# Attention's instructions within the expert steps get scheduler numbers 150 lower

## The chip, the cores and the metric

The kernel runs on one core of a Trainium2 chip. The metric is the device time of one execution in microseconds (us); the figure for a kernel is the median of its runs.

## The reference

Three layers run one after the other on 4 x 576 = 2304 tokens of 512 features. q, k and v come as 4 batches of 8 heads, 576 positions and 64 features.

```python
# 1 attention in a window of 64 positions
scores = q @ k.T / 8;  mask = (0 <= i - j < 64);  attn = softmax(scores where mask)
x = attn @ v                                   # heads side by side: 2304 x 512
# 2 first expert: w_in 512 x 2048, w_out 2048 x 512
h = x @ w_in
g = where(h >= 1, h, where(h <= -1, 0, (h + 1)**2 / 4))
x = g @ w_out
# 3 second expert: w_in 512 x 1024, w_out 1024 x 512
h = x @ w_in2;  s = h * softmax(h);  ln = (s - mean(s)) / sqrt(var(s) + 1e-6) * g_ln
out = ln @ w_out2
```

The weights `w_in` and `w_out` of both experts come as 64-bit numbers, everything else as float32.

## The kernel before

**Number format.** Every matmul of the two experts is made of three, with each operand split into a high and a low part (`xh`, `xl`; `wih`, `wil`; `woh`, `wol`; `gh`, `gl`): high x high, high x low, low x high. The 64-bit weights arrive in staging tiles `wst` (five of them) and are converted by five operations: L132 and L145 on ScalarE, L136, L137 and L146 on VectorE (`split_a`, `split_b`, `split_c`).

**Attention.** Tokens are cut into 12 tiles of 192 (index t). Up to t = 3 and a little beyond, the unit of work is a tile and two of the eight heads (index g, four units to a tile); later it is a pair of such units (index P). A unit goes through stages: q and k are loaded (`load_qk`, 8 transfers on SP's queue from t = 3 on, before that by whole tiles) and put into one of two buffers `kq` (`st_qkt`, by TensorE transposes for t < 3, by VectorE later); scores (`st_s`, `pair_s`: TensorE L352 or L442, then VectorE L360 or L452 for mask and maximum and ScalarE L366 or L458 for the exponential and its sum); normalising (`st_norm`, VectorE L377 to L386); transposes (`st_t`, TensorE L400 and L402, copied by ScalarE to `pT`); values (`st_v`, `pair_v`: TensorE L421 or L476, then ScalarE writes `xh` and VectorE `xl`, L428 and L429 or L483 and L484). In block 0 attention has two PSUM banks of its own and the experts' `ps_h` two; from block 1 on they share a ring of four. `p` has three buffers, `pT` two.

**First expert.** Tokens are taken in 6 blocks of 384 (index j), that is two tiles, and the hidden features in 16 groups of 128 (index f). A step (j, f) is 12 matmuls into `ps_h` (`moe_h`, L496, which read `xh[j]` and `xl[j]`), five operations for the activation (`moe_g`, `moe_g2`, `moe_g3`: ScalarE L505, L506, L512, VectorE L511, L515) and 12 matmuls into four accumulators (`moe_y`, L526), which are written in the program two steps later. At the end of a block the accumulators go to memory (`moe_out`). `xh` and `xl` have two buffers each, for the block in work and the next one. Block 0 is started in halves: its first two groups are done for its first 192 tokens, then for the other 192.

**How the two are interleaved.** The first seven units of attention are traced before the experts. The rest is a generator, `slots()`, which yields after each small stage. The step loop calls `slot(n0)` after a step's `moe_h` and `slot(n1)` after its `moe_y`; both are one slot in most steps, and eight slots are spread over the first two half steps. So a unit takes four slots, or two steps; a pair takes eight slots, or four steps. The last values stage for block 1 (unit 15) is the 38th of the 40 slots that fall in block 0. In block 0 each step also holds two weight conversions (`w_conv`) and two weight loads (`w_load`, SP's queue).

**What sets the order.** The kernel is written in Tile: the program as traced gives each instruction a number, and a scheduler fixes beforehand each engine's own order. Among the instructions of an engine whose inputs and buffers it takes to be ready, it picks the lowest number. On the chip each engine, and each DMA queue, keeps to the order so fixed. A few instructions are tied to others by hand (`tc.issue_after`).

**Second expert.** During blocks 1 to 5 its weights are converted as well (`w2_step`, partly on GpSimd). It begins inside block 5 and is alone from about 525 us on (the last L526 starts at 525.0).

Of the kernel before, what the change touches and what calls it, by code (L numbers as in the profile page):

```python
# [20 lines left out]
def kernel(  # L21
# [578 lines left out]
    def slots():  # L600
        for g in range(G0 + 1, GB + 1):
            st_s(g)
            yield
            st_v(g - 1)
            st_norm(g)
            yield
            qkt_and_loads(g + 1)
            v_ahead(g)
            yield
            st_t(g)  # L610
            if g == GB:
                st_s(g + 1)
            yield
        st_norm(GB + 1)
        qkt_and_loads(2 * PU)
        yield
        st_v(GB)
        st_t(GB + 1)
        qkt_and_loads(2 * PU + 1)
        yield  # L620
        for P in range(PU, NPP + 1):
            if P == PU:
                st_v(GB + 1)
            else:
                pair_v(P - 1)
            if P % NPR == 0:
                v_ahead(2 * P)
            if P < NPP:
                pair_s(P)
            yield  # L630
            if P < NPP:
                st_norm(P, 0)
                st_norm(P, 1)
            yield
            qkt_and_loads(2 * P + 2)
            yield
            qkt_and_loads(2 * P + 3)
            yield
            yield
            yield  # L640
            if P < NPP:
                st_t(P, 0)
                st_t(P, 1)
            yield
            yield

    stages = slots()

    def slot(n):
        for _ in range(n):  # L650
            next(stages, None)

    TPN = NB // 128
    NK2 = DF2 // 128
# [192 lines left out]
    for n in range(len(seq) + 2):  # L847
# [29 lines left out]
        if n < len(seq):  # L877
            prev = part
            slot(n0)
            w_conv()  # L880
            pins = moe_g2(*part)
# [5 lines left out]
        if n < len(seq):  # L887
            slot(n1)
            w_conv()
            if j == 0:  # L890
                w_load(2)
            w2_step(n, *pins)
            if last and f < 2:
                w2_vals(f)
            if last and f in (2, 3):
                w2_sums(f - 2)
            if last and f >= 2:
                with tc.issue_after(pins[0]):
                    w2_split(f - 2)
            if last and 2 <= f < 10:  # L900
                w2_load(f - 2)
        else:
            w_conv()
# [82 lines left out]
```

## Time and profile before

| | |
|---|---|
| median of 3 runs | 709.37 us (708.8 to 710.54) |
| the profiled execution | 709.96 us, span 708.2 us, mean granted TensorE clock 0.99 |
| TensorE matmuls (PE) | busy 683.4 us (96%), 4439 instructions |
| TensorE weight loads (PEld) | 629.5 us (89%) |
| VectorE (DVE) | 446.9 us (63%) |
| ScalarE (ACT) | 411.8 us (58%) |
| GpSimd (POOL) | 116.1 us (16%) |

The profile is of one execution. Its span goes from the first to the last instruction; the execution's own time is 1.8 us longer. Busy time is the share in which an engine works on an instruction; matmuls overlap each other and their weight loads, so a busy TensorE says that it had work, not that it ran at its peak. The granted clock is the share of full speed that TensorE was given: 1.00 is 2.4 GHz, 0.5 is 1.2 GHz. SP is the engine that issues most transfers.

### The profile page before, as it was taken

To read this page: it belongs to the slowest core of one execution; us is meant where nothing else is said; L and a number is where in the kernel's file an instruction comes from. 1 tells how busy PE (TensorE), PEld (TensorE's weight loads), DVE (VectorE), ACT (ScalarE), POOL (GpSimd) and SP (SyncE) were. 2 spreads that over 40 slices of the span, in tenths; PEclk is the share of its full clock that TensorE was granted. 3 is DMA by queue.
4 is the path that set the end of the run, shared out by engine and by line. 5 is a ranking of instruction groups with operands and counts; after the bars stand their busy time and mean duration, and the time that the engine had idled before them with its cause. 6 is when DMAs were issued, how large, how long until landed. Compare 5 with 4: busy or idle time off the path is not lost.

```text
span 708.2 us, 12544 instructions
## 1 busy us (share of the span) xinstructions
PE 683.4 (96%) x4439; PEld 629.5 (89%) x4439; DVE 446.9 (63%) x1213; ACT 411.8 (58%) x1006; POOL 116.1 (16%) x151
## 2 busy tenths in 40 slices
PE   6899898899999999999999999999999999999998
PEld 5799787799999999999999999999987788888887
DVE  4789788655545544454555543642379999988850
ACT  5889667465656555566666665364454646445451
POOL 1000000100001000021111200662272222220000
PEclk9999999899999999999999999999999999999999
DMA  9996787624343623447342211553024455533331
GB/s 199 224 259 193 193 213 199 154 40 105 71 107 79 148 60 67 80 104 148 96 89 81 85 60 60 171 180 110 1 84 140 149 187 163 188 132 133 120 105 45
DMA packets 155543, 88.94 MB, mean 126 GB/s; under 512 B 118616, under 2 KB 141400, under 8 KB 155480
## 3 DMA queue, kind: packets, MB, share of 16 engines
q1 hardware_dynamic: 144040, 64.00, 36.5%
q0 software_dynamic: 8704, 19.41, 8.4%
q10 hardware_dynamic: 2736, 4.72, 1.8%
q8 instruction: 35, 0.57, 0.3%
q14 instruction: 28, 0.23, 0.1%
HBM read 63.97 MB, written 24.12 MB: 124 GB/s over the span
## 4 chain that ended last, share of the span: by engine, by line
PE 75%; DVE 9%; issue 5%; DMA 4%; ACT 4%; POOL 2%; SPq 0%; DVEq 0%; POOLq 0%; ACTq 0%
PE ps_h L496 23%; PE acc L526 22%; PE ps_o L825 13%; PE P L710 8%; DMA wst<-in_moe_w_out_dram 2%; PE ps_x L476 2%; POOL wil L249 2%; PE ps_p L402 2%; PE ps_s L442 2%; PE ps_s L352 2%; DVE gl L515 1%; DVE wst L137 1%; ACT p L366 1%; DMA wst<-in_moe_w_in_dram 1%; PE ps_x L421 1%
## 5 line engine op out<-in xcount | busy, mean ns | idle before, releaser
L511 DVE SCALAR_TENSOR_TENSOR u<-u,ps_h 128x384 f32<-128x384 f32 (+1 forms) x98 | 53.2, 543 | 140.7 <-ACT u L506 139.7
L496 PE MATMUL ps_h<-xh,wih 128*128 128x384 f32 (+1 forms) x392 | 132.7, 339 | 1.3 <-DVE u L511 0.9
L526 PE MATMUL acc<-gl,woh 128*128 128x384 f32 (+1 forms) x392 | 130.6, 334 | 2.3 <-DVE gl L515 2.3
L496 PE MATMUL ps_h<-xl,wih 128*128 128x384 f32 (+1 forms) x392 | 131.7, 336 | 0.5 <-DVE xl L429 0.4
L496 PE MATMUL ps_h<-xh,wil 128*128 128x384 f32 (+1 forms) x392 | 132.0, 337 | 0.1
L526 PE MATMUL acc<-gh,wol 128*128 128x384 f32 (+1 forms) x392 | 129.5, 332 | 0.0
L526 PE MATMUL acc<-gh,woh 128*128 128x384 f32 (+1 forms) x392 | 125.3, 343 | 3.3 <-ACT gh L512 3.3
L505 ACT ACTIVATE u<-ps_h,half 128x384 f32<-128x384 f32 (+1 forms) x98 | 56.1, 573 | 95.2 <-PE ps_h L496 95.0
L515 DVE TENSOR_TENSOR gl<-u,gh 128x384 fp32r<-128x384 f32 (+1 forms) x98 | 61.3, 627 | 37.6 <-ACT gh L512 37.1
L512 ACT CAST gh<-u 128x384 fp32r<-128x384 f32 (+1 forms) x98 | 49.6, 507 | 51.4 <-DVE u L511 34.1
L526 PEld LDWEIGHTS acc<-gh,woh 128*128 128x128 f32 x392 | 72.2, 188 | 6.8 <-ACT gh L512 3.8
L496 PEld LDWEIGHTS ps_h<-xh,wih 128*128 128x128 f32 x392 | 74.9, 191 | 2.4 <-DVE u L511 1.1
L526 PEld LDWEIGHTS acc<-gl,woh 128*128 128x128 f32 x392 | 73.7, 188 | 3.6 <-DVE gl L515 3.4
L496 PEld LDWEIGHTS ps_h<-xl,wih 128*128 128x128 f32 x392 | 74.9, 191 | 1.0 <-DVE xl L429 0.8
L496 PEld LDWEIGHTS ps_h<-xh,wil 128*128 128x128 f32 x392 | 74.9, 191 | 0.8 <-DVE wil L146 0.7
L526 PEld LDWEIGHTS acc<-gh,wol 128*128 128x128 f32 x392 | 73.6, 188 | 0.1
L710 PE MATMUL P<-wih,x2p 128*128 128x512 f32 x216 | 70.7, 391 | 1.4 <-DVE xo L538 0.9
L825 PE MATMUL ps_o<-woh,wol 128*128 128x512 f32 (+1 forms) x152 | 57.7, 380 | 0.3 <-DVE wol L813 0.3
L825 PE MATMUL ps_o<-woh,woh 128*128 128x512 f32 (+1 forms) x152 | 57.7, 379 | 0.0
L825 PE MATMUL ps_o<-wol,woh 128*128 128x512 f32 (+1 forms) x152 | 57.5, 378 | 0.0
L506 ACT ACTIVATE u<-u 128x384 f32<-128x384 f32 (+1 forms) x98 | 51.0, 520 | 2.0
L710 PEld LDWEIGHTS P<-wih,x2p 128*128 128x128 f32 x216 | 40.5, 188 | 10.4 <-DVE xo L538 1.3
(122 smaller groups left out, 1175.9 us busy)
## 6 DMA issues: line engine op xcount, KB each, us to landing
vw<-in_v_dram SPq DMA_DIRECT2D x32, 256.0 KB, 5.2
wst<-in_moe_w_in_dram SPq DMA_DIRECT2D x16, 512.0 KB, 5.7
wst<-in_moe_w_out_dram SPq DMA_DIRECT2D x16, 512.0 KB, 5.3
lnd<-e SPq DMA_DIRECT2D x16, 512.0 KB, 2.6
lT<-lnd SPq DMA_DIRECT2D x64, 128.0 KB, 3.0
x2d<-xo POOLq DMA_DIRECT2D x24, 192.0 KB, 2.7
out_dram<-o ACTq DMA_DIRECT2D x17, 256.0 KB, 2.0
wst<-in_moe_w_in_dram POOLq DMA_DIRECT2D x8, 512.0 KB, 5.4
```

The source lines that it names most:

```text
L249: nc.gpsimd.tensor_tensor(lo, v_, as_f32(hi), op=ALU.subtract)
L352: nc.tensor.matmul(ps[:, i * 128 + c0:i * 128 + 128], qT[g][:, i, :, :].rearrange("p x q -> p (x q)"), kT[g][:, i * 64 + c0:i * 64 + 128], ...
L402: nc.tensor.transpose(ps[:, i * 128:i * 128 + 128], p[:, i, :], ident)
L496: nc.tensor.matmul(ps, a, bb[:, kc, c], start=(n == 0), stop=(n == 3 * KC - 1))
L505: nc.scalar.activation(u, ps, ACTF.Relu, bias=half, scale=0.5)
L506: nc.scalar.activation(u, u, ACTF.Square)
L511: g = nc.vector.scalar_tensor_tensor(u, u, 1.0, ps, op0=ALU.min, op1=ALU.max)
L512: return nc.scalar.copy(hi, u).ins, g.ins
L515: nc.vector.tensor_tensor(lo, u, as_f32(hi), op=ALU.subtract)
L526: nc.tensor.matmul(acc[j, e][:, c], a, bb, start=(f == 0 and n == 0 and c.start == 0), stop=(f == NF - 1 and n == 2),)
L710: nc.tensor.matmul(ps, l, r, start=(n == 0), stop=(n == 5))
L825: nc.tensor.matmul(ps, a[kk // 4][:, kk % 4, :], b[kk][:, c:c + w], start=(n == 0), stop=(n == 3 * NK2 - 1),)
```

## The change

`tc.high_priority(150)` lowers the number from which the scheduler counts by 150 for what is traced inside it, and puts it back on leaving. It is set around each slot of attention in the step loop. The stages of the first seven units, traced before the loop, are left as they are, and so is everything on GpSimd.

```diff
     def slot(n):
         for _ in range(n):
-            next(stages, None)
+            with tc.high_priority(150):
+                next(stages, None)
```

## Rows read from the trace of the kernel before

**Rows 1.** Stretches: us; busy PE, PEld, DVE, ACT, POOL (instructions); granted clock; DMA share; GB/s.
```profile
25.00:60.00 35.00, 31.80 (x279) 29.14 (x277) 29.97 (x100) 31.21 (x97) 0.00 (x0) 0.95 0.96 229
60.00:130.00 70.00, 63.38 (x403) 58.75 (x402) 58.45 (x164) 51.55 (x129) 1.25 (x2) 0.98 0.71 182
130.00:142.00 12.00, 9.17 (x57) 7.79 (x56) 6.79 (x29) 4.92 (x21) 2.70 (x5) 0.72 0.87 211
136.00:142.00 6.00, 5.75 (x21) 5.52 (x21) 2.29 (x11) 1.74 (x7) 0.34 (x1) 0.51 1.12 273
142.00:430.00 288.00, 288.00 (x2243) 278.78 (x2243) 148.81 (x480) 174.73 (x462) 32.44 (x47) 1.00 0.38 89
430.00:545.00 115.00, 112.24 (x624) 106.04 (x623) 61.46 (x102) 55.01 (x106) 50.71 (x50) 1.00 0.33 106
```
**Rows 2.** TensorE in order of time, 130 to 151 us: start, us, instruction, [idle before].
```profile
130.45 0.71 PE L421 MATMUL ps_x<-pT,vw 64*64 64x64 f32 x12
...
132.84 0.71 PE L421 MATMUL ps_x<-pT,vw 64*64 64x64 f32 x12
136.25 0.87 PE L402 MATMUL ps_p<-ident,p 128*128 128x128 f32 x3 [2.70 <-DVE p L386]
...
138.06 0.67 PE L496 MATMUL ps_h<-xh,wih 128*128 128x384 f32 x1
...
142.08 0.57 PE L421 MATMUL ps_x<-pT,vw 128*64 128x64 f32 x12
...
148.31 0.33 PE L496 MATMUL ps_h<-xh,wih 128*128 128x384 f32 x1
...
150.39 0.34 PE L526 MATMUL acc<-gl,woh 128*128 128x384 f32 x1
```
**Rows 3.** TensorE in order of time, three earlier places.
```profile
46.79 0.45 PE L496 MATMUL ps_h<-xh,wih 128*128 128x384 f32 x1 [0.91 <-DVE u L511]
...
119.07 0.83 PE L352 MATMUL ps_s<-kq 128*128 128x64 f32 x6
...
127.38 0.83 PE L352 MATMUL ps_s<-kq 128*128 128x64 f32 x6
```
**Rows 4.** Groups by line, ScalarE, whole span: count | busy us, mean ns | idle before.
```profile
L407 ACT COPY pT<-ps_p 128x384 f32<-128x384 f32 (+1 forms) x48 | 21.0, 440 | 2.4 <-PE ps_p L402 2.4
L366 ACT ACTIVATE p<-p,mx 128x128 f32<-128x128 f32 (+1 forms) x54 | 20.9, 390 | 5.0 <-DVE mx L360 4.9
...
L366 ACT ACTIVATION_READ_ACCUMULATOR p<-p,mx 128x1 f32 x54 | 10.4, 193 | 0.0
...
L428 ACT CAST xh<-ps_x 128x192 fp32r<-128x192 f32 x18 | 5.7, 314 | 0.9 <-PE ps_x L421 0.7
...
L339 ACT COPY kq<-ps_t 128x256 f32<-128x256 f32 (+1 forms) x12 | 4.3, 355 | 0.2
...
L338 ACT COPY kq<-ps_t 64x192 f32<-64x192 f32 x12 | 3.8, 313 | 6.0 <-DVE kq L337 5.7
```
**Rows 5.** SP's queue in order of time, 46 to 82 us.
```profile
46.99 1.17 SPq L126 DMA_DIRECT2D wst<-in_moe_w_out_dram  x1
...
63.58 0.37 SPq L124 DMA_DIRECT2D wst<-in_moe_w_in_dram  x1
64.39 1.78 SPq L291 DMA_DIRECT2D qk<-in_q_dram  x4
...
79.45 2.24 SPq L291 DMA_DIRECT2D qk<-in_k_dram  x4
```
**Rows 6.** ScalarE, then TensorE, in order of time around 90 us.
```profile
89.05 0.69 ACT L132 ACTIVATE wst<-wst 128x512 f32<-128x512 f32 x1 [2.52 <-DMA wst<-in_moe_w_in_dram]
...
90.18 1.22 PE L526 MATMUL acc<-gh,woh 128*128 128x384 f32 x4 [2.36 <-ACT gh L512]
```
**Rows 7.** DMA issues: queue, count, KB each, median us from issue to landing.
```profile
wst<-in_moe_w_in_dram SPq DMA_DIRECT2D x16, 512.0 KB, 5.7
...
qk<-in_q_dram SPq DMA_DIRECT2D x144, 24.0 KB, 2.8
```

## The prediction

> **What bounds the kernel now.** The reader starts with the page's busy times (in the table above): TensorE is busy 683.4 of 708.2 us, so a reordering can only win what lies in the remaining 25 us and in stretches at the lower clock. The next view is the table of stretches, which says where these lie [rows 1]. From 142 to 430 us, where expert blocks 1 to 4 run with attention between their steps, TensorE has 288.00 us busy in 288.00, at full clock: whatever order the same matmuls come in, nothing is won there. Before it, TensorE idles 3.20 us of 25 to 60, 6.62 us of 60 to 130, and 2.83 us of the twelve from 130 to 142, where the granted clock falls to 0.72 and, in the last six, to 0.51, which is the 1.2 GHz level. After it, 2.76 us of 430 to 545.
>
> The third view, TensorE in order of time, says what the stretch 130 to 142 is [rows 2]. Block 0's last expert matmuls have been issued by 130.45. From there to 138.06 TensorE issues no expert matmul at all, only attention: the values of one unit, transposes, scores, the values of the next (132.84), then 2.70 us idle until VectorE has normalised (136.25), then transposes and scores again. At 138.06 the first step of block 1 starts, since its input xh[1], xl[1] is complete only now, and its twelve matmuls take 4.02 us (138.06 to 142.08); the same twelve a little later take 2.08 (148.31 to 150.39). So block 1 waits for attention: the last unit that block 1 needs comes after block 0's work has run out.
>
> Is attention late because of its place in the queues, or can it go no faster? Two scores stages near the end start at 119.07 and 127.38, so a unit takes 8.31 us; the last of these units has its values at 132.84, 5.46 us after its scores, and two units can be under way [rows 2, 3]. It is its place that sets the pace, and this place is what the change alters.
>
> **The change part by part.** Nothing is removed or added: every instruction of the slots gets a number 150 lower, all else keeps its own. It moves the slots' matmuls on TensorE, their passes on VectorE and ScalarE, and their q, k and v loads on SP's queue. They issue nothing on GpSimd's queue. How far? A step of block 0 numbers 24 matmuls, 5 operations of the activation, 10 of weight conversion and 2 loads, 41 in all, so 150 are 3.7 steps if attention's own instructions don't count, and about 2.5 if they do (some 19 a step, counted in the code). Block 0's fourteen whole steps lie between 46.79 and 130.45 us, 6.0 us a step [rows 2, 3]. Attention is to come 15 to 22 us earlier; it is late by 7.6 (130.45 to 138.06) [rows 2]. Both counts are enough; I take 3.7, that is 1.83 units (a unit is two steps).
>
> Gap A, 130 to 142. The idle time is 2.83 us [rows 1]. The clock: 5.75 us busy at 0.51 in 136 to 142 would be 2.93 at full clock, a loss of 2.82; the twelve matmuls alone show 1.94 of it [rows 1, 2]. Together 5.65 us. The attention matmuls in the gap have to be done anyway, only earlier. With xh[1] complete in time, block 1's first steps can fill TensorE while block 0's last activations finish. I take -5.65; the bounds are 0 (the gap only moves) and -5.65.
>
> Cost B, where the 1.83 units go. The first slots have nothing in front of them any more, so the lead is built from about 25 us on, as fast as units go through. On ScalarE a unit costs three exponentials at 0.390 with a sum read at 0.193 (1.75), the copy of the transposes (0.44), of xh (0.314) and two copies of q and k (0.313 and 0.355): 3.17 us, 5.80 for the lead [rows 4]. ScalarE has 35.00 - 31.21 = 3.79 us free in 25 to 60, VectorE 5.03 [rows 1]. So about 2.0 us of weight conversion is pushed back on ScalarE, which is the tighter one. TensorE has attention's matmuls to do meanwhile, so I take half, +1.0. The bounds are 0 and the whole 5.80 as idle time of TensorE, if the conversions are what each step is waiting for.
>
> Loads, on SP's queue. Between 48.16 and 63.58 SP issues four loads, 1.42 us of work: 14.0 us free. Then, from 64.39 to 81.69, the 24 loads of three units come in one burst with weight loads between them, at 14.5 us of issue, 0.61 each [rows 5]. The lead moves some 15 of them forward, 9 us, which fits into the free stretch. What it would cost otherwise is in the trace as well: at 89.05 ScalarE has waited 2.52 us for a weight transfer, the cast of gh stands behind that wait on its queue, and TensorE waits 2.36 us for gh [rows 6]. I take 0 for the loads. The bounds are a second such wait, +2.36, and a gain of 4.0: half of the 6.62 us idle in 60 to 130 and of the 1.4 that the clock of 0.98 costs there [rows 1], if the burst no longer meets weight loads that are needed at once.
>
> Here a rule of the Trainium skill speaks against the change. The transfers that move are small: 24 KB takes 2.8 us to land where 512 KB of weights takes 5.7, some ten times as long per byte [rows 7]. The skill ("DMA: Bandwidth & Descriptors", section Specifications) says that transfers below 512 B don't reach line rate, and the code's q and k rows are 128 B long; by it, weights in flight beside these loads come later, wherever the burst stands. If that makes one more wait of 2.36 us, the sum below is -2.3, and 707.7 us.
>
> Blocks 1 to 4. A unit can't write xh[j+2] before block j's last step has read xh[j], as the pool has two; so at the start of each block the lead shrinks to about a step and is built again. A unit that is issued as soon as its inputs are due could find them late; the nearest row is the 2.70 us wait at 136.25 [rows 2]. Against it stands that 2243 matmuls ran there without any idle time [rows 1], and that what is overdue at a block's start is a values stage and transposes whose inputs lie ready. I take 0; the bounds are 0 and 4 x 2.70 = 10.8.
>
> The rest. Attention ends some 20 us earlier, so the memory that the second half needs comes free earlier; 430 to 545 has 2.76 us idle [rows 1], and I take 0, with bounds of half of that either way.
>
> The sum against the profiled execution, 709.96 us: -5.65 + 1.0 = -4.65, so 705.3 us. This execution is 0.6 us above the median of the three runs (709.37), less than their spread, so the forecast stands at 705.3. What a measurement of this kernel can tell from no change is about 0.3%, 2.1 us.
>
> **The rivals.** First, weights late (slower). Attention's passes stand ahead of the weight conversions on ScalarE and VectorE. For it speaks that these two are 89% and 86% busy in 25 to 60; against it, that TensorE idles only 3.20 us there and gets attention's matmuls in return. If all 5.80 us turn into idle time, with one fall of the clock like the one priced in A (2.82), the sum is -5.65 + 5.80 + 2.82 = +2.97: 712.9 us. It decides as soon as TensorE's idle time and clock losses in 25 to 130 grow by more than 5.65 us.
>
> Second, the gap moves (same). The 5.80 us become idle time without a fall of the clock, or attention is held by its buffers (two banks, two kq, three p), so that the numbers hardly change the order and the change doesn't do what it says: 709.96 to 710.1 us. Against the buffers speaks the pace above.
>
> Third, waits in the steady stretch (slower): 10.8 us once a block, 709.96 - 4.65 + 10.8 = 716.1 us. Only the early rows speak for it.
>
> Fourth, the middle of block 0 gains too (faster): another 4.0 us, 701.3.
>
> **How the numbers follow.** Forecast 0.46, weights late 0.17, gap moves 0.20, waits in the steady stretch 0.07, middle gains 0.10. The forecast's own range is 703 to 708; a small part of it (0.03) lies within 0.3%. Faster is 0.43 + 0.10 = 0.53, same 0.20 + 0.03 = 0.23, slower 0.17 + 0.07 = 0.24. The range goes from the fourth rival, 701.0, to the first, 713.0; the third and the far ends of the first and fourth are left out.
>
> **What would show it.** In the changed kernel's trace, TensorE in order of time: the values stage of block 1's last unit stands before block 0's last expert matmuls, the first matmul of block 1 follows them without a stretch of attention alone, and the granted clock there stays at 1.00. ScalarE is busier than 31.21 us in 25 to 60, and the L291 loads of the burst begin before 64.39. The stretch 142 to 430 stays without idle time. The prediction is wrong if block 0's conversions (L132, L137) end later by more than the gap was long, if TensorE waits for gh or wih in 25 to 130 for over 9.8 + 5.65 us, or if p, pT or xl shows up among TensorE's waits after 142.

## The result and the profile after

The changed kernel takes 712.12 us in the median of 18 runs (710.02 to 714.97), the kernel before 708.22 us in 18 runs on the same chip (706.32 to 711.02). The ratio is 1.0054 with a 95% interval of 1.0039 to 1.0069: 3.9 us slower, where 705.3 us and faster was the forecast. The profiled execution of the changed kernel took 712.17 us (span 710.4), close to its median; that of the kernel before, 709.96 us, was 1.7 us over this median. So the two traces show only 2.2 us of the 3.9.

The stretches of [rows 1] without 136 to 142, and two more (57 to 71 and 525 to 535 us), in the changed kernel:

```profile
25.00:60.00 35.00, 32.32 (x296) 29.07 (x296) 30.14 (x108) 32.83 (x106) 0.00 (x0) 0.96 0.96 236
57.00:71.00 14.00, 14.00 (x104) 13.33 (x104) 13.86 (x38) 12.19 (x33) 0.00 (x0) 1.00 0.40 85
60.00:130.00 70.00, 61.20 (x373) 56.73 (x372) 59.24 (x166) 49.73 (x124) 1.25 (x2) 0.93 0.72 186
130.00:142.00 12.00, 12.00 (x91) 11.23 (x89) 5.48 (x18) 6.15 (x18) 0.00 (x0) 1.00 0.53 99
142.00:430.00 288.00, 288.00 (x2234) 278.55 (x2234) 151.71 (x481) 175.27 (x462) 35.07 (x52) 1.00 0.38 93
430.00:545.00 115.00, 110.29 (x610) 104.71 (x610) 60.20 (x98) 55.07 (x105) 50.40 (x50) 0.99 0.31 104
525.00:535.00 10.00, 6.63 (x23) 4.93 (x22) 6.44 (x14) 2.59 (x5) 5.11 (x8) 0.83 0.72 238
```

Gap A is gone: 130 to 142 us is full and at full clock. Two things pay for it. Between 60 and 130 us TensorE has 61.20 us busy at a clock of 0.93, where it had 63.38 at 0.98 [rows 1]; with 25 to 60, idle time and clock losses (share missing times length) grow from 12.97 to 17.78 us; by the same count the gap had cost 6.19 us. And the stretch 525 to 535 us has fallen. In the kernel before, the two added stretches were:

```profile
57.00:71.00 14.00, 14.00 (x94) 13.35 (x93) 13.62 (x37) 13.65 (x32) 0.00 (x0) 1.00 0.63 173
525.00:535.00 10.00, 9.08 (x41) 7.23 (x40) 7.65 (x16) 3.93 (x8) 5.83 (x10) 1.00 0.79 238
```

**The front: weights late.** SP's queue in order of time in the changed kernel, to be read beside [rows 5]:

```profile
56.50 0.37 SPq L124 DMA_DIRECT2D wst<-in_moe_w_in_dram  x1
57.60 1.78 SPq L291 DMA_DIRECT2D qk<-in_q_dram  x4
59.44 1.98 SPq L291 DMA_DIRECT2D qk<-in_k_dram  x4
...
67.91 2.73 SPq L291 DMA_DIRECT2D qk<-in_k_dram  x4
70.74 0.39 SPq L126 DMA_DIRECT2D wst<-in_moe_w_out_dram  x1
71.22 0.39 SPq L124 DMA_DIRECT2D wst<-in_moe_w_in_dram  x1
...
116.53 0.39 SPq L126 DMA_DIRECT2D wst<-in_moe_w_out_dram  x1
```

And in the kernel before, two weight loads of the same stretch and block 0's last one:

```profile
58.86 0.34 SPq L126 DMA_DIRECT2D wst<-in_moe_w_out_dram  x1
...
66.29 0.37 SPq L126 DMA_DIRECT2D wst<-in_moe_w_out_dram  x1
...
112.60 0.39 SPq L126 DMA_DIRECT2D wst<-in_moe_w_out_dram  x1
```

The 24 loads of three units now go back to back from 57.60 to 70.64 us, and no weight load stands between 56.50 and 70.74. In the kernel before, weight loads went out at 56.13, 58.86, 63.58 and 66.29 us. While SP issues these 24 to 32 KB transfers, the DMA engines are busy 0.40 of 57 to 71 us at 85 GB/s, where it was 0.63 at 173. The delay is not made up: block 0's last weight load goes out 3.9 us later.

What a late weight does is seen 40 us on, first on ScalarE, then on TensorE (number in brackets: us waited, and for what):

```profile
107.71 0.69 ACT L132 ACTIVATE wst<-wst 128x512 f32<-128x512 f32 x1 [1.54 <-DMA wst<-in_moe_w_in_dram]
108.29 0.57 ACT L505 ACTIVATE u<-ps_h,half 128x384 f32<-128x384 f32 x1
108.75 0.64 ACT L145 CAST wih<-wst 128x512 fp32r<-128x512 f32 x1
...
120.40 0.71 ACT L132 ACTIVATE wst<-wst 128x512 f32<-128x512 f32 x1 [0.61 <-DMA wst<-in_moe_w_in_dram]
120.99 0.59 ACT L505 ACTIVATE u<-ps_h,half 128x384 f32<-128x384 f32 x1
121.45 0.53 ACT L512 CAST gh<-u 128x384 fp32r<-128x384 f32 x1
```

```profile
109.45 0.44 PE L496 MATMUL ps_h<-xh,wih 128*128 128x384 f32 x1 [3.05 <-ACT wih L145]
...
122.03 0.96 PE L526 MATMUL acc<-gh,woh 128*128 128x384 f32 x4 [2.60 <-ACT gh L512]
```

The pass that waits for a landing weight (L132) holds the cast of an older weight (L145) behind it on the in-order engine, and TensorE waits 3.05 us for that cast. The second wait is the chain of [rows 6] with a shorter wait for the transfer (0.61 us): the cast of gh stands behind it. ScalarE's waits for landing weights as a whole hardly grew, 15.1 us in 60 to 130 where the kernel before has 14.2; what grew is what TensorE waits for wih, from 0.3 to 3.8 us in 25 to 142. Block 0's last step runs its pass L511 at 134.5 us in place of 126.1, and block 1's first one at 142.5 in place of 143.5. That last 1.0 us is within the scatter of single executions, as runs 1, 2, 7 and 8 show below.

**Attention: ahead, but for its last unit.** The last two values stages that block 1 needs, then VectorE's normalising for the second of them, in the changed kernel:

```profile
114.34 0.71 PE L421 MATMUL ps_x<-pT,vw 64*64 64x64 f32 x12
...
130.34 0.71 PE L421 MATMUL ps_x<-pT,vw 64*64 64x64 f32 x12
```

```profile
118.89 0.16 DVE L377 TENSOR_SCALAR sm<-sm 128x3 f32<-128x3 f32 x1
...
124.40 0.42 DVE L386 TENSOR_TENSOR p<-p,rs 128x256 f32<-128x256 f32 x1
```

The first of them comes 16.1 us earlier than in the kernel before (114.34 for 130.45), the second only 2.5 (130.34 for 132.84) [rows 2]. Its normalising takes from 118.89 to 124.82 us, since weight conversions (L136, L137, L146), some of them waiting for their weights, stand between its four passes on VectorE; in the kernel before the four took 0.95 us.

**The tail: one bank.** The two profiled executions reach the tail within 0.5 us of each other: the first copy of the last block's sums (L536) starts at 524.47 us before, at 524.02 after. From there to the end of the span it is 183.73 us before and 186.38 after. The changed kernel's TensorE, then VectorE (lines from L652 on are one higher than before):

```profile
525.09 0.40 PE L711 MATMUL P<-wih,x2p 128*128 128x512 f32 x1
528.86 0.51 PE L711 MATMUL P<-wih,x2p 128*128 128x512 f32 x1 [3.37 <-DVE stat L740]
```

```profile
524.76 1.24 DVE L779 TENSOR_SCALAR s<-s,stat 128x1024 f32<-128x1024 f32 x1 [0.46 <-POOL stat L775]
526.03 1.25 DVE L791 STREAM_TRANSPOSE e<-s 128x1024 f32<-128x1024 f32 x1
527.20 0.98 DVE L538 COPY xo<-acc 128x384 f32<-128x384 f32 x2
528.11 0.67 DVE L740 CUSTOM_DVE_ANT_0 s<-P,u 128x512 f32<-128x512 f32 x1
```

The next product (P1) waits for VectorE to read the last one (P3, L740), and that reading stands behind three other pieces of work. The built programs say why: the last ring tiles got PSUM banks P4:0, P2:2, P3:3 in the kernel before and P4:3, P2:2, P3:0 after, and the pool behind the ring gives its first product (P1) bank 0 in both. TensorE's order is the same in both programs over the last third of its instructions; only the ring of four banks has arrived by another rotation. In the kernel before, all six matmuls of P1 go out here at once, and TensorE waits for the bank of the product behind it, and briefly:

```profile
528.24 0.50 PE L710 MATMUL P<-wih,x2p 128*128 128x512 f32 x1 [0.92 <-DVE xo L538]
```

### The profile page after: what moved, and what is told of

Same layout as the page of the kernel before. It is cut to its first block, busy times and chain, and to the rows that moved or that the text cites. A ratio compares the mean times of both kernels' runs of the same rounds, so it can differ in the third digit from the quotient of the medians.

```text
span 710.4 us, 12537 instructions
## 1 busy us (share of the span) xinstructions
PE 683.5 (96%) x4439; PEld 629.6 (89%) x4439; DVE 449.2 (63%) x1213; ACT 413.2 (58%) x1006; POOL 115.7 (16%) x151
## 4 chain that ended last, share of the span: by engine, by line
PE 77%; DVE 6%; DMA 6%; issue 5%; ACT 3%; POOL 2%; SPq 1%; POOLq 0%; DVEq 0%
PE ps_h L496 22%; PE acc L526 22%; PE ps_o L826 14%; PE P L711 11%; DMA wst<-in_moe_w_out_dram 3%; PE ps_x L476 2%; POOL wil L249 2%; DMA wst<-in_moe_w_in_dram 2%; PE ps_s L442 2%; PE ps_p L402 2%; PE ps_s L352 1%; SPq L291 1%; DVE gl L515 1%; DVE p L360 1%; PE ps_x L421 1%
## 5 line engine op out<-in xcount | busy, mean ns | idle before, releaser
L496 PE MATMUL ps_h<-xl,wih 128*128 128x384 f32 (+1 forms) x392 | 134.2, 343 | 1.3 <-DVE xl L429 1.1
L511 DVE SCALAR_TENSOR_TENSOR u<-u,ps_h 128x384 f32<-128x384 f32 (+1 forms) x98 | 53.2, 544 | 122.8 <-ACT u L506 122.1
L526 PE MATMUL acc<-gh,woh 128*128 128x384 f32 (+1 forms) x392 | 121.5, 335 | 2.6 <-ACT gh L512 2.6
L711 PEld LDWEIGHTS P<-wih,x2p 128*128 128x128 f32 x216 | 41.3, 191 | 12.3 <-DVE stat L740 3.8
```

What stands on the lines that cost most here:

```text
L496: nc.tensor.matmul(ps, a, bb[:, kc, c], start=(n == 0), stop=(n == 3 * KC - 1))
L511: g = nc.vector.scalar_tensor_tensor(u, u, 1.0, ps, op0=ALU.min, op1=ALU.max)
L526: nc.tensor.matmul(acc[j, e][:, c], a, bb, start=(f == 0 and n == 0 and c.start == 0), stop=(f == NF - 1 and n == 2),)
L711: nc.tensor.matmul(ps, l, r, start=(n == 0), stop=(n == 5))
```

## The experiments

Each ratio is to runs of the kernel before on the same chip; runs 1 to 4, 5 to 8, 9 to 12 and 13 to 16 were on four different chips. The marks are of the one profiled execution: L511 of block 0's last step and of block 1's first, then the first L536 of the last block, and what is left of the span after it.

| run | ratio (95% interval) | L511 marks | last block | rest |
|---|---|---|---|---|
| kernel before | | 126.1, 143.5 | 524.47 | 183.73 |
| changed | 1.0054 (1.0039 to 1.0069) | 134.5, 142.5 | 524.02 | 186.38 |
| 1: changed, other bank | 1.0032 (1.0016 to 1.0049) | 136.2, 144.2 | 525.84 | 183.96 |
| 2: before, same bank | 1.0040 (1.0022 to 1.0057) | 123.8, 139.9 | 522.11 | 185.59 |
| 3: stages only | 1.0081 (1.0057 to 1.0104) | 126.9, 147.6 | 528.17 | 183.73 |
| 4: loads only | 1.0048 (1.0026 to 1.0070) | 136.0, 146.3 | 526.65 | 183.75 |
| 5: changed, weights on GpSimd | 1.0087 (1.0062 to 1.0112) | 129.3, 149.3 | 529.95 | 183.75 |
| 6: before, weights on GpSimd | 1.0179 (1.0155 to 1.0203) | 135.1, 154.9 | 535.91 | 183.89 |
| 7: raised from block 1 | 1.0020 (1.0002 to 1.0037) | 125.0, 143.1 | 523.68 | 183.72 |
| 8: raised in block 0 | 1.0046 (1.0026 to 1.0065) | 136.2, 143.3 | 525.64 | 183.76 |
| 9: changed, 21 weights on GpSimd | 0.9936 (0.9915 to 0.9957) | 127.8, 139.8 | 520.46 | 183.54 |
| 10: before, 21 weights on GpSimd | 0.9985 (0.9965 to 1.0005) | 122.8, 142.4 | 524.02 | 183.48 |
| 11: changed, weights raised too | 1.0050 (1.0031 to 1.0070) | 125.9, 145.8 | 526.15 | 183.75 |
| 12: before, weights raised | 1.0030 (1.0010 to 1.0049) | 122.6, 143.3 | 524.96 | 183.74 |
| 13: as 9, same bank | 0.9963 (0.9943 to 0.9983) | 124.2, 136.1 | 516.73 | 184.57 |
| 14: as 9, loads only | 0.9972 (0.9953 to 0.9991) | 121.2, 138.8 | 519.86 | 183.54 |
| 15: as 9, stages only | 0.9922 (0.9899 to 0.9945) | 123.5, 137.1 | 517.65 | 183.55 |
| 16: as 9, raised by 300 | 0.9953 (0.9928 to 0.9979) | 126.4, 139.3 | 519.93 | 183.57 |

**The bank alone (1 and 2).** One more ring tile (N = 2), or three more (N = 4), in the second block:

```diff
-                ps = at_bank("ps_g")
-                nc.tensor.transpose(ps[:, 0:DF2 // 128], gl_row, ident[...])
-                nc.vector.tensor_copy(gl_sb, ps[:, 0:DF2 // 128])
+                for z in range(N):
+                    ps = at_bank("ps_g")
+                    nc.tensor.transpose(ps[:, 0:DF2 // 128], gl_row, ident[...])
+                    nc.vector.tensor_copy(gl_sb[:, 2 * z:], ps[:, 2 * z:DF2 // 128])
```

In run 2, and from run 4 on, the copies begin at column z, not 2 * z.

> The changed kernel with one more tile taken from the ring of four PSUM banks in the first block after the ring opens (the 8 columns of the gain are transposed into two ring tiles in place of one, half of the columns read from each: 0.2 us of work). It moves the ring on by a place: the last product of the first pool (P3) gets bank 1 and the first product of the pool behind it (P1) gets bank 0, which P4 had. Theory BANK (of the 3.9 us lost, 2.65 is one bank: P1 waits at 528.86 for VectorE's reading of P3 because both sit in bank 0): the wait of 3.37 is gone, the stretch 525 to 535 again has about 9 us of TensorE at a clock of 1.00, and the time is about 709.5, 1.2 over before. Theory FRONT (all of it is lost in block 0, and 525 to 535 only reflects it): 712.1, as the changed kernel. Theory SPEED (the tail waits because attention ended earlier and VectorE is late with the rest): the wait stays in another bank, 712.

> The kernel before, nothing raised, with three more tiles taken from the ring of four PSUM banks in the same place (the gain's columns are transposed four times, a quarter read from each: 0.5 us of work). It moves the ring so that P3 and the first P1 of the pool behind both sit in bank 0, as in the changed kernel. Theory BANK: a wait of about 3.4 us on VectorE's L740 at the first P product behind the last L526, a clock under 0.9 in the 10 us behind it, and 2.65 us more: 710.9. Theories FRONT and SPEED: as before, 708.2.

Run 1, stretches and TensorE:

```profile
525.00:535.00 10.00, 9.08 (x43) 7.41 (x42) 7.68 (x16) 3.52 (x9) 7.00 (x10) 1.00 0.61 205
```

```profile
529.62 0.50 PE L711 MATMUL P<-wih,x2p 128*128 128x512 f32 x1 [0.92 <-DVE xo L538]
```

Run 2, TensorE:

```profile
526.36 0.79 PE L710 MATMUL P<-wih,x2p 128*128 128x512 f32 x1 [2.77 <-DVE stat L739]
```

With the bank moved, the wait for L740 is gone and the stretch is as before; with the shared bank put into the kernel before, the wait comes there, the rest of the span is 1.86 us longer, and 525 to 535 us has a clock of 0.83. So the wait belongs to the bank; FRONT alone and SPEED fall. The last column of the table says the same: the rest of the span is 184.57 to 186.38 us in the three kernels with the shared bank (changed, 2, 13) and 183.48 to 183.96 in the fifteen others. By the ratios the bank is worth 0.0022 in the changed kernel (1.6 us) and 0.0040 in the kernel before (2.8), with intervals that reach over each other. But 2.3 us of loss stay in run 1, and BANK's 709.5 us is missed: what is left is lost elsewhere.

The marks of these runs also show how far single executions scatter. TensorE's order up to block 1's first matmul is the same in the kernel before and in runs 2 and 7, and the same in the changed kernel and in runs 1 and 8. With the old order block 1's first L511 comes at 139.9 to 143.5 us, with the new at 142.5 to 144.2: no gain. Idle time and clock losses in 25 to 130 us are 9.3 to 13.0 us with the old order and 17.8 to 21.3 with the new, 8.2 more on average; in 130 to 142 they are 4.3 to 6.3 and 0, 5.6 less. That leaves a loss of 2.7 us in the front, in line with run 1.

**What of the raise costs in the front (3 and 4).** Run 3 puts the loads back within the stage, run 4 raises them alone (both with N = 2 as above, where banks would else be shared, as in all runs below):

```diff
     def slot(n):            # run 3 keeps it, run 4 has no raise here
         for _ in range(n):
             with tc.high_priority(150):
                 next(stages, None)
...
+        with tc.high_priority(-150):      # run 4: 150
             if m >= NPE and m + 4 < NG:
                 load_qk(m + 4)
...
+            with tc.high_priority(-150):  # run 4: 150
                 load_v(t + 1)
```

> The computing stages of attention alone are raised by 150; its loads of q, k and v keep their old numbers (raised back by 150 the other way within the stage). One more ring tile as in the first experiment, so that P3 (bank 3) and P1 (bank 0) differ. Theory LOAD (in block 0 the raised loads stand ahead of the weight loads on SP's queue, the last weight load is issued 3.9 us later, and this eats what the gap at 130 to 142 gives back): weight loads between the q/k loads again, last one at about 112.6, stretch 60 to 130 at 63 us of TensorE and a clock of 0.98, the gap at 130 to 142 still closed: 708.2 - 5.65 + 1 = 703.5. Theory CONV (attention's passes on ScalarE and VectorE, now ahead of the weights' conversion, are what holds TensorE up in block 0): as the changed kernel without the bank's wait, 709.5.

> The loads of q, k and v alone are raised by 150; the computing stages keep their old numbers. One more ring tile, P3 in bank 1 and P1 in bank 0. Theory LOAD: 24 loads of q and k in a row on SP's queue with no weight load between, block 0 later by about 3.9 us and nothing won: 710 to 712. Theory CONV: as before, 708.2.

Run 3, then run 4, stretches:

```profile
60.00:130.00 70.00, 63.21 (x396) 58.12 (x396) 57.55 (x151) 49.74 (x117) 1.25 (x2) 0.98 0.75 189
130.00:142.00 12.00, 8.21 (x75) 6.72 (x74) 7.92 (x37) 6.54 (x27) 2.71 (x5) 0.91 0.63 165
```

```profile
60.00:130.00 70.00, 59.43 (x374) 54.29 (x373) 57.91 (x166) 49.65 (x124) 1.25 (x2) 0.90 0.75 188
130.00:142.00 12.00, 12.00 (x84) 11.51 (x84) 7.65 (x28) 7.39 (x24) 0.00 (x0) 1.00 0.49 91
```

Neither theory is right. The raised loads alone make the weights late (last one 119.22 us) and close the gap, as LOAD says; CONV's "as before" falls. But with the loads left behind, the weights are in time (last one 113.10) and the gap stays: attention doesn't get ahead. Its copies of the transposes that start at 80.4 and 92.4 us in run 1 start at 87.3 and 107.5 in run 3. That is 1.0081, the worst of these four, where LOAD expected 703.5 us. Yet no engine waits for q or k. The scores that run 3 starts at 86.27 us read a kq that was written 13 us before; TensorE's fixed order has them behind expert matmuls, which waited 1.70 and 1.49 us:

```profile
72.75 0.38 DVE L326 STREAM_TRANSPOSE kq<-qk 128x192 f32<-128x192 f32 x1
```

```profile
86.27 0.83 PE L352 MATMUL ps_s<-kq 128*128 128x64 f32 x6
```

ScalarE's waits for landing weights in 70 to 110 us tell nothing here: they are 12.3 us in run 3, 11.6 in the kernel before and 11.3 in the changed one. After this, theory SUM (a fixed sum of passes on ScalarE and VectorE) was the rival.

**Where it is lost (5 to 8).** Runs 5 and 6 issue all 32 weight loads from GpSimd's queue; runs 7 and 8 raise by place:

```diff
-        return w_unit(src, hi, lo)
+        return w_unit(src, hi, lo, None, nc.gpsimd)                     # 5, 6
...
-            with tc.high_priority(150):
+            with (tc.high_priority(150) if j else ExitStack()):         # 7; the other way round in 8
```

> The changed kernel with the first expert layer's 32 weight loads issued from GpSimd's DMA queue, in place of SP's, and one more ring tile, so that P3 (bank 3) and the first P1 (bank 0) differ. The raised loads of q and k can no longer stand ahead of a weight load in a queue. Theory LOAD: the weight loads go out at their old times or earlier (last one at 112.6 or before), the step that ends block 0 is no longer held up by ScalarE's wih, and the gap at 130 to 142 stays closed: 708.2 - 5.65 + 1 = 703.5. Theory SUM (formed after the last runs: in block 0 ScalarE and VectorE owe a fixed sum of passes, conversions and attention, before block 1 can start; which goes first only decides which end waits): as the same kernel with the loads on SP's queue, 710.5 to 711.2, block 1 starting at 143 to 144 as there.

> The kernel before with the first expert layer's weight loads on GpSimd's DMA queue, nothing else changed (banks as before). It says what the other queue is worth alone. Theory LOAD: the weights were in time before, attention was late, so the gap at 130 to 142 stays: 708.2 within 1. Theory SUM: the same, 708.2.

> Attention is raised by 150 only within the expert steps from the second block on; block 0 keeps its old numbers. One more ring tile, P3 (bank 3) and P1 (bank 0) differ. If all that is lost outside the bank is lost in block 0 (theories LOAD and SUM alike), the front is as in the kernel before, with its gap at 130 to 142, and the 1.1 us that the changed kernel wins between 223 and 524 (300.77 against 301.88) stay or are spent in block 1, where attention gets ahead: 707 to 708.2. If raising costs something in the later blocks too (theory SPREAD): over 709.

> Attention is raised by 150 only within block 0; later blocks keep their numbers. The banks fall apart by themselves (P3 in bank 1, P1 in bank 0). Theories LOAD and SUM: the whole loss of the front, no gain later: 711 to 712, with block 1 starting at 143 to 144. Theory SPREAD: 708 to 709.

Runs 5 and 6 missed both forecasts: the first L511 runs at 45.4 and 46.7 us, before at 34.4. The first weights don't go out late (1.98 us in run 5, 6.86 before). But GpSimd also makes attention's mask, and the weight loads now stand ahead of the mask's last step in its order; it runs at 14.79 us in run 5, before at 2.08, and VectorE waits for it:

```profile
14.79 0.64 POOL L76 TENSOR_SCALAR_AFFINE_SELECT mask<-mask 64x128 f32<-64x128 f32 x2
```

```profile
15.47 0.23 DVE L360 CUSTOM_DVE_ANT_0 p<-ps_s,mask 128x64 f32<-128x64 f32 x1 [5.82 <-POOL mask L76]
```

Between the two, though, the raise is worth 0.0092, 6.5 us, a gain (1.3 us of it may be the earlier start); that spoke against SUM. Run 8 carries the front's loss (1.0046, no shared bank), run 7 little: 1.0020, at the edge of what can be told. Its 709.77 us lies on SPREAD's side of the forecasts, but "nothing" isn't ruled out.

**Weights on a queue of their own (9 and 10).** The first 11 loads stay on SP, so the start is as before:

```diff
-        return w_unit(src, hi, lo)
+        return w_unit(src, hi, lo, None, nc.sync if len(wdma) < 11 else nc.gpsimd)
```

> The changed kernel with the first 11 weight loads left on SP's queue and the other 21 (those of the expert steps) on GpSimd's, so that the start stays as it was (with all 32 there the first expert step began 11 us later). One more ring tile, P3 in bank 3 and P1 in bank 0. Theory LOAD: the weights are out by 112.6, ScalarE's and VectorE's waits for landing weights (15.1 and 6.6 us in 60 to 130) shrink, block 1's first pass L511 starts at 138 to 140 in place of 142.5: 704 to 706. Theory SUM: a fixed sum of passes, block 1 at 143 to 144: 710.5.

> The kernel before with the same 21 weight loads on GpSimd's queue, nothing raised; one more ring tile, P3 in bank 2 and P1 in bank 0. The control of the run with the raise. Theory LOAD: weights were in time, so only the q/k loads gain a little from the freed SP queue; the gap at 130 to 142 mostly stays: 707 to 708.5, so that the raise is worth 3 to 4 us where it can't push the weights back. Theory SUM: 708, and the raise worth nothing or a loss.

Run 9, stretches, then ScalarE's waits in 60 to 130 us (us in all, times, longest):

```profile
60.00:130.00 70.00, 66.11 (x436) 61.04 (x436) 62.99 (x171) 54.62 (x136) 13.02 (x20) 1.00 0.79 201
130.00:142.00 12.00, 11.08 (x109) 9.76 (x109) 7.21 (x27) 7.22 (x24) 2.72 (x5) 1.00 0.73 168
```

```profile
ACT wst L132 <- DMA wst<-in_moe_w_in_dram: 4.3, 5, 2.0
...
ACT wst L132 <- DMA wst<-in_moe_w_out_dram: 2.2, 4, 1.4
```

This is the run that decides. The same raise on the same stages, with the weights in a queue of their own: 703.05 us, 0.9936. The last weight load goes out at 111.92 us, ScalarE waits 6.5 us for landing weights where the changed kernel waited 15.1, the kernel before 14.2 and run 10 8.7, TensorE has 66.11 us busy at full clock in 60 to 130, and the gap is nearly closed. The second queue alone (run 10) is worth 0.0015, not to be told from nothing; the raise is worth 0.0049 on top, 3.5 us, where with one queue it cost 2.3 (run 1). SUM falls: the passes are the same. The order on every engine was fixed anew for each of these programs, so what is compared is the two streams in one queue or in two, with the order that follows from it. The Trainium skill says ("Trainium Kernel Development and Optimization", section Key Constraints) that issuing DMAs from several engines' queues only saves the sequencer's issue time, as all run on the same DMA engines. The runs agree with it, and show what that "only" was worth beside this raise: 6.8 us between runs 1 and 9 (by their ratios, on two chips).

**One queue in a better order (11 and 12).** The weight loads of block 0's steps are raised by 150 too, on SP's queue:

```diff
             if j == 0:
-                w_load(2)
+                with tc.high_priority(150):
+                    w_load(2)
```

> The changed kernel with the weight loads of block 0's expert steps raised by 150 as well, so that they stand among the raised q/k loads on SP's queue again. One more ring tile, P3 in bank 3 and P1 in bank 0. Theory LOAD: the last weight load is back at about 113, the waits of TensorE for ScalarE's wih (3.8 us) are gone, block 1 starts at 139 to 141: 705 to 707. Theory SUM: 710.5 to 711, as with the loads left behind.

> The kernel before with only block 0's weight loads raised by 150, attention not. Banks differ (P3 in bank 2, P1 in bank 0). Theory LOAD: the weights were not what block 0 waited for; attention's loads fall back and the gap at 130 to 142 stays or grows: 708 to 711. Theory SUM: 708.2.

Run 11, stretches:

```profile
60.00:130.00 70.00, 63.68 (x387) 57.83 (x386) 58.51 (x159) 49.98 (x121) 1.25 (x2) 0.98 0.72 182
130.00:142.00 12.00, 8.42 (x65) 6.76 (x65) 6.66 (x27) 5.34 (x20) 2.70 (x5) 0.78 0.83 208
```

LOAD's number for run 11 (705 to 707) is missed: the weights are back in time (last one 113.63 us, wait for wih 1.0), and with that the gap is back as well and block 1 starts at 145.8. Run 12 shows the same from the other side: the last weight load goes out at 107.08 us, the gap stays, at a clock of 0.50, and 2.1 us are lost. None of the orders tried on one queue (changed, 3, 4, 8, 11, 12) had both in time, where with two queues (9, 13, 15, 16) the weights were in time and block 1's first L511 came at 136.1 to 139.8 us; so LOAD's "the old order of the weights cures it" falls, and the two streams in one queue stay as the cause. For the weights the trace shows how: SP issues q and k while they stand behind. For attention it doesn't, as no engine waits for q or k in runs 3 and 11. That the scheduler placed its stages later because it reckoned with later loads would fit, and isn't shown.

**The price of the bank again, and which part wins (13 to 16).** Run 13 is run 9 without the extra ring tile; runs 14 and 15 are run 9 with the edits of runs 4 and 3; run 16 has 300 for 150.

> The kernel with the raise and the 21 later weight loads on GpSimd's queue, without the extra ring tile: P3 and the first P1 then both sit in bank 0; all else is as in that kernel (703.05). Theory BANK: a wait of about 3.4 us on VectorE's L740 before the first P product behind the last L526 and 2.65 us more: 705.7. If the bank were worth only what the clock of one profiled run showed: 703 to 704.

> The 21 later weight loads on GpSimd's queue and only the loads of q, k and v raised, the computing stages at their old numbers; banks differ (P3 in 3, P1 in 0). Theory LOAD (the q/k loads' place in SP's queue sets how fast attention goes in block 0; nothing is pushed back now): most of the 5 us, 704 to 705. If the raise of the stages is what wins once the weights are in time: 708, as without the raise.

> The 21 later weight loads on GpSimd's queue and only the computing stages raised, the loads of q, k and v at their old numbers; one more ring tile, P3 in bank 3, P1 in bank 0. With SP's queue holding almost nothing but q/k/v loads, their order there is the same as with all raised. Theory LOAD: as with all raised, 703 to 704. If the loads' numbers still matter: 706 to 708.

> The 21 later weight loads on GpSimd's queue and attention raised by 300 in place of 150; one more ring tile, P3 in bank 3, P1 in bank 0. If attention is still late at block 1's start (its first L511 at 139.8 behind a last one of block 0 at 127.8), more raise brings it 1 to 3 us nearer: 700 to 702. If by now the passes of ScalarE and VectorE are the bound: 703 or more.

Run 13, the stretch around the wait, and TensorE:

```profile
505.00:535.00 30.00, 26.61 (x129) 23.18 (x129) 23.71 (x46) 14.82 (x28) 17.57 (x20) 1.00 0.32 97
```

```profile
521.59 0.50 PE L711 MATMUL P<-wih,x2p 128*128 128x512 f32 x1 [3.39 <-DVE stat L740]
```

The same wait, 3.39 us, but the clock stays at 1.00, and the rest of the span is 1.0 us over that of run 9. The ratios differ by 0.0027, 1.9 us, with intervals that reach over each other. So the wait is certain, and its price lies between 1.0 and 2.7 us in the three traces, more in the two where the clock fell behind it. Runs 14 and 15: with the queues apart it is the stages' raise that wins (0.9922, about the 703 to 704 us of LOAD, with run 9 inside its interval); the loads' alone gives less (0.9972, 706.84 us, between its two forecasts). A raise by 300 gives no more: 705.39 us, on the side of "703 or more"; that the passes are then the bound wasn't looked at.

## Why the prediction was wrong

**Gap A (-5.65): right as a stretch, wrong as a gain.** The stretch 130 to 142 us is full, at a clock of 1.00, as the text said it would look. But block 1 starts no earlier (142.5 to 144.2 us for 139.9 to 143.5, three traces each), since block 0's last step came later (134.5 to 136.2 for 123.8 to 126.1). The gain was counted as if the work ahead of the gap would stay where it was. One reading was wrong as well: block 1's input was complete before 138.06, as its last pass on VectorE shows in the kernel before:

```profile
134.87 0.35 DVE L429 TENSOR_TENSOR xl<-ps_x,xh 128x192 fp32r<-128x192 f32 x1
```

After that block 1's first step stood in TensorE's order behind the transposes and scores of a later unit, which waited until 136.25 us for VectorE's L386. So attention was late by 4.8 us, not 7.6.

**How far (15 to 22 us): right for all but the last unit.** The values of the last but one came 16.1 us earlier, those of the last 2.5, in the changed kernel; block 1 needs both.

**Loads on SP's queue (0): the step that failed.** It said that the 15 moved loads, 9 us of issue, fit into 14.0 us in which SP issues little between 48.16 and 63.58. SP was not free there: its queue is served in order, and it stood waiting at the head for weight buffers (9.5 us at L124 for VectorE's L146 in 47 to 65 us). The loads moved from 64.39 to 57.60, and what they pushed back was the weight loads behind them. The bound of +2.36, one more wait like [rows 6], was the right mechanism at half the size: waits of 3.05 and 2.60. The rule of the Trainium skill weighed there is not what decided: over the whole span the median landing of a 24 KB q load is 2.8 us before and after, that of a weight (w_in) 5.7 and 5.6. The transfers were not slower, they were issued later.

**Cost B (+1.0): not what happened.** ScalarE is busier in 25 to 60 us, as foreseen (32.83 for 31.21), but TensorE has more work done there, not less (32.32 for 31.80). The cost fell in 60 to 130, and through late weights more than through passes in the way: the same passes with the same raise win 3.5 us in run 9 over run 10.

**Blocks 1 to 4 (0): right.** 288.00 us busy in 288.00; no p, pT or xl among the waits.

**The rest (0, within 1.4): the second step that failed.** 430 to 545 us lost 1.95 us of busy time and some clock, by a bank whose number nobody had set. Of its bounds neither held a wait of 3.37 us. Between the front and the tail, from block 1's first L511 to the last block's sums, attention's being ahead gives nothing that can be told: 380.5 to 381.7 us where the later blocks are raised (changed, 1, 3, 7), 380.3 to 382.4 where they aren't (before, 2, 4, 8).

**The rivals.** "Weights late", 712.9 us, came true by name, and almost in its time, but by another road: it spoke of conversions behind attention's passes, and they were conversions without weights. Nearness in time is in part luck, as the bank's share was in none of the rivals. Its own sign, losses in 25 to 130 us that grow by more than 5.65, is not met by the two profiled executions (4.81) and is met by the average of three each (8.2). Its chance was put at 0.17 because its price was looked for on ScalarE in 25 to 60 us, where nothing was lost. "The gap moves" describes the front well; it had been priced without the fall of the clock.

**The signs of being wrong.** None of the three came: the last L132 of block 0 started 4.5 us later in the changed kernel, less than the gap was long, TensorE waited 6.4 us for gh and wih in 25 to 130, and no p, pT or xl stands among its waits after 142. They were set too wide, and none of them looked at SP's queue or at the PSUM banks.

**The sum, as measured.** From the ratios: all but the bank +2.3 us (run 1, interval 1.1 to 3.5), which lies in the front by the losses counted above, and bank +1.6 (the changed kernel against run 1): 3.9. How much of the 3.9 each takes can't be told closer than about 1 us, since single executions of these two kernels lie up to 2.9 us from their median. Why run 3 and run 4 each lose more in the front than both raises together (run 1) stays open, and so does why the stages' raise alone goes from the worst on one queue to the best on two.

## What to carry to other kernels

Before moving a group of instructions up, list the DMA loads that move with it and what stands behind them in the same queue: a queue that issues little is not free if its head is waiting, and two streams with different due times belong in two queues, if the engine that issues the second has no work of its own that is needed early, as GpSimd had with the mask. Change the queue and the priority together; here the raise alone cost 3.9 us, the queue alone gave nothing to be told, and both gave 4.5 to 5.5. When a reordering in one stage makes a far stage slower without any change of order there, compare the buffers that a rotating pool handed out, at the boundary to the next pool above all.

## What the runs showed that was not expected

A PSUM bank shared by the last tile of one pool and the first of the next made TensorE wait 2.77 to 3.39 us; without it the wait at that place was 0.92. The Trainium skill's advice to let independent matmul groups rotate through different PSUM banks ("Perfetto Trace Analysis", section Matmuls) is borne out at this one place: the rotation was there, and the border between two pools broke it. The same wait of 3.4 us cost 2.66 us where the granted clock behind it was 0.83, and 1.0 us where it stayed at 1.00.

Issuing a 512 KB weight load of block 0's steps took GpSimd 0.54 to 0.96 us (run 9), where SP mostly needed 0.34 to 0.40. In run 9 TensorE waits for nothing on GpSimd after the start; with the first loads there too (runs 5 and 6) the mask came 12.7 and 14.6 us later, and with it the first expert step 11 to 12.
